# Three-stage kernel (attention, routed experts, gated convolution): one weight decoding, two decodings' last operations, one scaling and the routing's rest change place

## The chip, the cores and the metric

One core of a Trainium2 chip. The time is that of one execution on the device, in microseconds (us); the kernel before was run three times. The engines are TensorE (PE; PEld is its weight load), VectorE (DVE), ScalarE (ACT), GpSimd (POOL) and SyncE (SP, which only issues DMAs here). Each engine takes its instructions in the order of the program; engines wait for one another by semaphores.

## The reference

Three stages over 2 sequences of 768 tokens, 512 wide:

```python
state = gamma * state + outer(k[t], v[t]);  y[t] = scale * q[t] @ state      # 8 heads of 64
logits = x @ w_gate; local = sigmoid(x @ w_local)                             # 8 experts
e = argmax(logits[s]) if s == 0 or local[s] < 0.5 else prev_e                 # one expert per token
out[s] = softmax(logits[s])[e] * (relu(x[s] @ w1[e]) @ w2[e])                 # 512 -> 1024 -> 512
h = relu(x @ w_in); c = conv3(h, conv_w); y = (h * sigmoid(c)) @ w_out        # 512 -> 1024 -> 512
```

`w_in` and `w_out` arrive as 64-bit floats and have to be turned into 32-bit ones on the chip: the decoding. Matmuls are done as three products of split operands (a high and a low part of each; high x high, high x low, low x high).

## The kernel before, in words

The first stage goes over 12 tiles of 128 tokens and writes the tokens' rows to a scratch `scr` in DRAM; beside it the routing is worked out. In the second stage expert e gets 256 slots. Experts 1 to 6 run whole (`L1`, line 695, then `L2`, line 725); the first and the last run as two passes of 128 slots each (`alone`, line 629, a generator: each `yield` is a place at which the caller can put other work; n counts them). The third stage starts as soon as the rows of the first six tiles can be gathered.

Weights are loaded in units of 512 KB (`load_unit`, 4 buffers), split by a cast on ScalarE (line 172, `whi`) and a subtraction on VectorE (line 181, `wlo`), some 8 units ahead of their use. The subtraction's end lets SyncE issue the load that takes the buffer.

One decoding (`decode`, line 197; 16 in all) is: two reads on ScalarE (215, 216), five operations on VectorE (218 to 224), two on GpSimd (226 a product, 227 a sum). `dec_first` issues the two reads, `dec_second` the rest and then the next load of 64-bit data. The buffers `dmag`, `df` and `ds` exist once; decodings called with `mo` take others (`dmf`). 

The routing's rest (`route_rest`, line 549) is a generator of five pieces of 3 to 4 small VectorE operations, one piece with an exponential on ScalarE; it gives `posi`, the rows that the third stage gathers, and `G_all`, the factors by which it scales them (`c_scale`, on ScalarE for tile 4, on VectorE for tiles 0 to 3 and 5).

The order is written out by hand, instruction by instruction. Around the change it is: in the first expert's first pass the overflow's branch (line 836, not taken here), the gathers of expert 1, and the transposes T of the first expert's second half (lines 579 to 585: transposes on TensorE, cast `xsh` on ScalarE, subtraction `xsl` on VectorE). In the last expert's second pass the third stage's gathered tiles are scaled (`c_scale`), transposed and split (`c_T`, line 946) between the matmuls.

Of the kernel before, what the change touches and what calls it, by code (L numbers as in the profile page):

```python
# [8 lines left out]
F32 = mybir.dt.float32  # L9
# [5 lines left out]
ALU = mybir.AluOpType  # L15
# [5 lines left out]
DM = 512  # L21
# [76 lines left out]
def tile_kernel(ctx: ExitStack, tc: tile.TileContext, consts, qk, kv, w1, w2, w_in, conv_w, w_out, out):  # L98
    nc = tc.nc
# [94 lines left out]
    n_dec = KD + KF // 2  # L194
    wdec = [(dp if j < n_dec - KEPT else cst).tile([P, 1024], F32, name=f"wdec{j}") for j in range(n_dec)]

    def decode(raw64, out, pool=None, s=None):

        n, m = out.shape
        r3 = raw64.rearrange("p (c two) -> p c two", two=2)  # L200
        lo, hi = r3[:, :, 0], r3[:, :, 1]

        def tmp(name, dt):
            return dp.tile([P, DM], dt, name=name, tag=name)[0:n, 0:m]

        if pool is None:
            mag, f = tmp("dmag", F32), tmp("df", F32)
        else:
            both = pool.tile([P, 2, DM], F32, name="dmf", tag="ow", bufs=2)
            mag, f = both[0:n, 0, 0:m], both[0:n, 1, 0:m]  # L210
        s = (tmp("ds", F32) if s is None else s[0:n, 0:m]).bitcast(I32)
        a = mag.bitcast(I32)
        ve = nc.vector

        nc.scalar.activation(out=mag, in_=hi.bitcast(F32), func=AF.Abs)
        nc.scalar.activation(out=f, in_=lo.bitcast(U32), func=AF.Copy, scale=2.0 ** -52)
        yield
        ve.tensor_scalar(mag, mag, F64_LOW, F64_HIGH, op0=ALU.max, op1=ALU.min)
        ve.tensor_scalar(a, a, 4, -2 ** 31, op0=ALU.logical_shift_left, op1=ALU.bitwise_xor)
        yield  # L220
        ve.tensor_scalar(s, hi, -2 ** 31, None, op0=ALU.bitwise_and)
        ve.scalar_tensor_tensor(out=a, in0=a, scalar=1, in1=s, op0=ALU.logical_shift_right, op1=ALU.bitwise_or)

        ve.tensor_scalar(s, a, -2 ** 23, None, op0=ALU.bitwise_and)  # L224
        yield
        nc.gpsimd.tensor_tensor(out=f, in0=f, in1=s.bitcast(F32), op=ALU.mult)  # L226
        nc.gpsimd.tensor_tensor(out=out, in0=f, in1=a.bitcast(F32), op=ALU.add)  # L227

    dec_src = []
    for dt in range(KD):  # L230
# [4 lines left out]
    dec_raw = {}  # L235
# [8 lines left out]
        queue.dma_start(out=t, in_=dec_src[u].bitcast(I32))  # L244
        dec_raw[u] = t

    def dec_first(pool=None, s=None):
        dec_second()
        u = dnx["run"]
        if u >= len(dec_src):  # L250
            return
        dnx["run"] += 1
        dec_raw["g"] = decode(dec_raw.pop(u), wdec[u // 2][:, (u % 2) * DM:(u % 2 + 1) * DM], pool, s)
        next(dec_raw["g"])

    def dec_second(queue=nc.sync):
        if "g" in dec_raw:
            for _ in dec_raw.pop("g"):
                pass
            dec_load(queue)  # L260
# [17 lines left out]
    x0 = cst.tile([P, DM], F32, name="x0")  # L278
# [154 lines left out]
    last = {"cnt": base}  # L433
# [169 lines left out]
    def moe(mo):  # L603
# [11 lines left out]
        def T(e, halves=(0, 1)):  # L615
            if e not in xs_t:
                xs_t[e] = (mo.tile([P, KD, CAP], F32R, name="xsh", tag="xsh", bufs=1),
                           mo.tile([P, KD, CAP], F32R, name="xsl", tag="xsl", bufs=1))
            for half in halves:
                sl = slice(half * P, (half + 1) * P)  # L620
                transposed(xg_t[e].pop(half), *(x[:, :, sl] for x in xs_t[e]))
# [73 lines left out]
        def L1(e):  # L695
            xh, xl = xs_t.pop(e)
            hh, hl = h_tiles(e)
            pb = [bank("b") if j < 3 else std for j in range(KF // 2)]
            for dt in range(KD):
                wh, wl = split[e * 8 + dt]  # L700
                if dt == 0:
                    dec_second()
                elif dt == 1:
                    next(rest, None)
                elif dt == 2:
                    dec_first(mo)
                for ft in range(KF):
                    o = pb[ft // 2][:, (ft % 2) * CAP + OFF:(ft % 2 + 1) * CAP]
                    fs = slice(ft * P, (ft + 1) * P)

                    for n, (a, b_) in enumerate(((wh, xh), (wl, xh), (wh, xl))):
                        nc.tensor.matmul(o, lhsT=a[:, fs], rhs=b_[:, dt, OFF:], start=(dt == 0 and n == 0 and ft % 2 == 0),  # L712
                                         stop=(dt == KD - 1 and n == 2), skip_group_check=True)
                    if dt == KD - 1 and ft % 2:
                        fp = ft // 2
                        dst = hh[:, 2 * fp:2 * fp + 2, OFF:]
                        pair = pb[fp].rearrange("p (a t) -> p a t", a=2)[:, :, OFF:]
                        nc.scalar.activation(out=dst, in_=pair, func=AF.Relu)  # L718
                        nc.vector.scalar_tensor_tensor(out=hl[:, 2 * fp:2 * fp + 2, OFF:], in0=pair, scalar=0.0,  # L719
                                                       in1=dst.bitcast(F32), op0=ALU.max, op1=ALU.subtract)  # L720
                split.pop(e * 8 + dt)
                if dt < KD - 1:
                    split_unit(nc.vector)
# [53 lines left out]
            pass  # L777
        rest = route_rest()
        for n, _ in enumerate(first):
            if n in (0, 1, 2, 5):  # L780
                split_unit(nc.vector)
            if n == 5:
                T(0, (1,))
            if n == 3:
                overflow(mo)
                gather(1)
            if n == 5:
                dec_first()
            elif n == 7:
                dec_second()  # L790
        for n, _ in enumerate(alone(0, 1, True)):
            if n == 0:
                dec_first()
            elif n == 1:
                dec_second()
            if n == 9:
                T(1, (0,))
            elif n == 11:
                T(1, (1,))
                gather(2)  # L800
# [10 lines left out]
        for n, _ in enumerate(alone(e, 0, False)):  # L811
            if n in (0, 8, 13):
                dec_second()
            elif n == 5:
                dec_first()
            elif n == 9:
                dec_first(mo, x0)
        raw0 = [dp.tile([P, 2, DM], F32, name="yg0", tag="draw", bufs=2) for _ in range(2)]
        ygs = [raw0[c // 2][:, c % 2, :] for c in range(4)] + [x_last.rearrange("p a t -> p (a t)"), x0]
        for c in range(NC):  # L820
# [2 lines left out]
        for n, _ in enumerate(alone(e, 1, True)):  # L823
            if 8 <= n < 12:
                c_scale(n - 8)
            if n == 7:
                window(1, [wp.tile([P, 1024], F32R, name="x2", tag=tag) for tag in ("whi", "whi", "wlo", "wlo")])
            if 10 <= n < 14:
                c_T(0, n - 10, "ab"[n % 2])
            if n == 12:  # L830
                c_scale(4)
            if n == 13:
                c_scale(5)

    def overflow(mo):
# [413 lines left out]
```

## Time and profile before

| | |
|---|---|
| median of 3 runs | 410.25 us (409.18 to 411.04) |
| the profiled execution's own time | 409.37 us |
| its span, first to last instruction | 407.6 us |
| mean granted TensorE clock | 0.996 |
| TensorE busy | 391.4 us (96%) |
| VectorE busy | 286.8 us (70%) |
| ScalarE busy | 246.6 us (60%) |
| GpSimd busy | 117.8 us (29%) |

TensorE is busy nearly all of the span, the others are not; so the table says little of which of them matters where. For that one looks at the few stretches in which TensorE stands still, and at the granted clock in them. Times in the rows below are us from the span's start.

### The profile page before, as it was taken

To read this page: it belongs to the slowest core of one execution; us is meant where nothing else is said; L and a number is where in the kernel's file an instruction comes from. 1 tells how busy PE (TensorE), PEld (TensorE's weight loads), DVE (VectorE), ACT (ScalarE), POOL (GpSimd) and SP (SyncE) were. 2 spreads that over 40 slices of the span, in tenths; PEclk is the share of its full clock that TensorE was granted. 3 is DMA by queue.
4 is the path that set the end of the run, shared out by engine and by line. 5 is a ranking of instruction groups with operands and counts; after the bars stand their busy time and mean duration, and the time that the engine had idled before them with its cause. 6 is when DMAs were issued, how large, how long until landed. Compare 5 with 4: busy or idle time off the path is not lost.

```text
span 407.6 us, 7354 instructions
## 1 busy us (share of the span) xinstructions
PE 391.4 (96%) x2772; PEld 339.0 (83%) x2772; DVE 286.8 (70%) x544; ACT 246.6 (60%) x483; POOL 117.8 (29%) x110
## 2 busy tenths in 40 slices
PE   7999998979999999999999999799999999999996
PEld 4888876658989797998989777599979889998986
DVE  3368867957797999987877857659963736991350
ACT  4887752646855766576757563478864537981431
POOL 3455510264035153564744246532000000000000
PEclk9999999989999999999999999999999999999999
DMA  8999992868878797988979130533010010001002
GB/s 289 396 351 407 325 347 92 239 232 284 308 244 277 270 318 255 290 298 277 304 246 304 53 101 26 156 90 92 0 51 27 0 54 27 2 0 51 27 0 77
DMA packets 28087, 73.24 MB, mean 180 GB/s; under 512 B 3009, under 2 KB 3649, under 8 KB 28050
## 3 DMA queue, kind: packets, MB, share of 16 engines
q1 hardware_dynamic: 19506, 54.67, 39.1%
q10 hardware_dynamic: 6240, 10.55, 7.2%
q0 software_dynamic: 2304, 7.54, 6.0%
q8 instruction: 22, 0.36, 0.4%
q14 instruction: 15, 0.12, 0.1%
HBM read 62.26 MB, written 10.49 MB: 178 GB/s over the span
## 4 chain that ended last, share of the span: by engine, by line
PE 66%; DVE 17%; ACT 6%; DMA 5%; issue 4%; POOL 1%; ACTq 0%; DVEq 0%; POOLq 0%
PE c L1045 15%; PE b L993 11%; PE c L744 11%; DVE wlo L181 6%; PE rt L993 5%; PE b L712 4%; PE c L406 2%; PE b L652 2%; PE state L712 2%; PE rt L712 2%; PE b L346 2%; ACT whi L172 2%; DMA raw<-in_moe_w_dram 2%; PE a L374 2%; DMA C<-in_consts_dram 1%
## 5 line engine op out<-in xcount | busy, mean ns | idle before, releaser
L181 DVE TENSOR_TENSOR wlo<-raw,whi 128x1024 fp32r<-128x1024 f32 x64 | 82.1, 1295 | 18.4 <-ACT whi L172 17.6
L172 ACT CAST whi<-raw 128x1024 fp32r<-128x1024 f32 x64 | 66.7, 1055 | 40.6 <-PE c L744 21.9
L1012 DVE SCALAR_TENSOR_TENSOR cs<-hs,cw,cs 128x384 f32<-128x384 f32 x64 | 39.6, 619 | 30.6 <-ACT cs L1010 29.0
L226 POOL TENSOR_TENSOR dmf<-dmf,ds 128x512 f32<-128x512 f32 x12 | 24.9, 2076 | 83.5 <-DVE ds L224 50.1
L744 PE MATMUL c<-whi,hh 128*112 128x512 f32 x96 | 38.0, 395 | 0.3 <-ACT hh L718 0.3
L993 PE MATMUL b<-x,whi 128*128 128x386 f32 x176 | 37.1, 340 | 0.8 <-ACT x L960 0.8
L744 PE MATMUL c<-wlo,hh 128*112 128x512 f32 x96 | 37.5, 390 | 0.0
L1045 PE MATMUL c<-whi,gh 128*128 128x512 f32 x88 | 35.1, 399 | 0.0
L1045 PE MATMUL c<-whi,gl 128*128 128x512 f32 x88 | 34.9, 396 | 0.0
L1045 PE MATMUL c<-wlo,gh 128*128 128x512 f32 x88 | 34.7, 395 | 0.0
L993 PEld LDWEIGHTS b<-x,whi 128*128 128x128 f32 x176 | 31.2, 189 | 1.4 <-ACT x L960 1.2
L744 PE MATMUL c<-whi,hl 128*112 128x512 f32 x96 | 29.8, 392 | 0.6 <-DVE hl L719 0.6
L611 POOL DMA_INDIRECT xg<-scr,permi x15 | 20.3, 1353 | 26.5 <-DVE nbi L541 19.6
L712 PE MATMUL b<-xsl,whi 128*128 128x240 f32 x96 | 26.6, 277 | 0.4 <-DVE xsl L585 0.4
L712 PE MATMUL b<-xsh,whi 128*128 128x240 f32 x96 | 26.5, 276 | 0.0
L712 PE MATMUL b<-xsh,wlo 128*128 128x240 f32 x96 | 26.4, 275 | 0.0
L352 DVE TENSOR_TENSOR A<-b,mask 128x512 f32<-128x512 f32 x24 | 15.4, 685 | 11.1 <-PE b L346 11.1
L227 POOL TENSOR_TENSOR wdec<-dmf 128x512 f32<-128x512 f32 x13 | 22.8, 1757 | 1.0
L1016 ACT ACTIVATE sg<-cs 128x384 f32<-128x384 f32 x32 | 16.6, 519 | 9.1 <-DVE gl L1022 8.5
L744 PEld LDWEIGHTS c<-whi,hl 128*112 128x112 f32 x96 | 17.2, 181 | 5.8 <-DVE hl L719 1.5
L744 PEld LDWEIGHTS c<-whi,hh 128*112 128x112 f32 x96 | 17.4, 181 | 4.9 <-ACT hh L718 0.6
L744 PEld LDWEIGHTS c<-wlo,hh 128*112 128x112 f32 x96 | 17.4, 181 | 4.2
(251 smaller groups left out, 1015.9 us busy)
## 6 DMA issues: line engine op xcount, KB each, us to landing
raw<-in_moe_w_dram SPq DMA_DIRECT2D x64, 512.0 KB, 4.8
qk<-in_qk_dram SPq DMA_DIRECT2D x11, 512.0 KB, 6.6
kv<-in_kv_dram SPq DMA_DIRECT2D x11, 512.0 KB, 6.6
draw<-in_moe_w_in_dram SPq DMA_DIRECT2D x8, 512.0 KB, 3.6
draw<-in_moe_w_out_dram SPq DMA_DIRECT2D x8, 512.0 KB, 3.3
scr<-xo ACTq DMA_DIRECT2D x11, 256.0 KB, 8.1
out_dram<-os ACTq DMA_DIRECT2D x11, 256.0 KB, 2.0
scr<-ys ACTq DMA_DIRECT2D x10, 256.0 KB, 4.2
```

What stands on the lines that cost most here:

```text
L172: nc.scalar.copy(hi, raw[u])
L181: engine.tensor_tensor(out=lo, in0=t, in1=hi.bitcast(F32), op=ALU.subtract)
L226: nc.gpsimd.tensor_tensor(out=f, in0=f, in1=s.bitcast(F32), op=ALU.mult)
L227: nc.gpsimd.tensor_tensor(out=out, in0=f, in1=a.bitcast(F32), op=ALU.add)
L352: nc.vector.tensor_tensor(out=A_t[i][j], in0=sc2[j].rearrange("p (a t) -> p a t", a=NP), in1=mask.unsqueeze(1).to_broadcast([P, NP, P]), o ...
L611: nc.gpsimd.indirect_dma_start(out=t, out_offset=None, in_=xrow, in_offset=bass.IndirectOffsetOnAxis(ap=permi[:, col:col + 1], axis=0))
L712: nc.tensor.matmul(o, lhsT=a[:, fs], rhs=b_[:, dt, OFF:], start=(dt == 0 and n == 0 and ft % 2 == 0), stop=(dt == KD - 1 and n == 2), skip ...
L744: nc.tensor.matmul(yp[t][0:P - o], lhsT=a[:, ft, t * P + o:(t + 1) * P], rhs=b_[:, ws], start=(ft == 0 and a is hh and b_ is wh), stop=(ft ...
L993: nc.tensor.matmul(pb[:, 0:WN], lhsT=split[u_in + dt][wi][:, fs], rhs=x_[dt // 2][:, dt % 2, :], start=(n == 0), stop=(n == 3 * KD - 1))
L1012: nc.vector.scalar_tensor_tensor(out=cs, in0=tap[j], scalar=cw[:, j, ft:ft + 1], in1=cs, op0=ALU.mult, op1=ALU.add)
L1016: nc.scalar.activation(out=sg, in_=cs, func=AF.Sigmoid)
L1045: nc.tensor.matmul(ops[t][:, 0:n_], lhsT=a[:, ts_], rhs=b_[:, ws], start=(ft == 0 and n == 0), stop=(ft == KF - 1 and n == 2))
```

## The change

`decode` gets an argument `last`, the engine of its two last operations (226 and 227): GpSimd unless said otherwise, VectorE for the two decodings of the last expert's first pass. In the first expert's first pass the first decoding's reads are issued at n = 3 behind the gathers instead of at n = 5 behind T, its other operations at n = 4 instead of n = 7, and the split that stood at n = 5 now stands at n = 7; T stays at n = 5. `L1` no longer runs a piece of the routing's rest; `L2` does as before. In the last expert's second pass the scaling of tile 4 moves from n = 12 to n = 13, behind the transposes and casts of that step; the scaling of tile 5 stays at n = 13.

```diff
-    def decode(raw64, out, pool=None, s=None):
+    def decode(raw64, out, pool=None, s=None, last=nc.gpsimd):
...
-        nc.gpsimd.tensor_tensor(out=f, in0=f, in1=s.bitcast(F32), op=ALU.mult)
-        nc.gpsimd.tensor_tensor(out=out, in0=f, in1=a.bitcast(F32), op=ALU.add)
+        last.tensor_tensor(out=f, in0=f, in1=s.bitcast(F32), op=ALU.mult)
+        last.tensor_tensor(out=out, in0=f, in1=a.bitcast(F32), op=ALU.add)
...
@@ L1
                 if dt == 0:
                     dec_second()
-                elif dt == 1:
-                    next(rest, None)
                 elif dt == 2:
                     dec_first(mo)
...
@@ first expert, first pass
         for n, _ in enumerate(first):
-            if n in (0, 1, 2, 5):
+            if n in (0, 1, 2, 7):
                 split_unit(nc.vector)
-            if n == 5:
-                T(0, (1,))
             if n == 3:
                 overflow(mo)
                 gather(1)
-            if n == 5:
                 dec_first()
-            elif n == 7:
+            elif n == 4:
                 dec_second()
+            elif n == 5:
+                T(0, (1,))
...
@@ last expert, first pass
             elif n == 5:
-                dec_first()
+                dec_first(last=nc.vector)
             elif n == 9:
-                dec_first(mo, x0)
+                dec_first(mo, x0, nc.vector)
...
@@ last expert, second pass
-            if n == 12:
+            if n == 13:
                 c_scale(4)
-            if n == 13:
                 c_scale(5)
```

## Rows read from the trace of the kernel before

**Rows 1.** TensorE's waits, whole span: who waited for whom, us, times, longest.
```profile
PE a L640 <- ACT hr L663: 3.2, 2, 3.0
PE a L950 <- DVE yg L942: 2.5, 1, 2.5
...
PE c L744 <- DVE hl L719: 0.6, 2, 0.5
```

**Rows 2.** Timeline, TensorE, first expert: start, duration, operation, [idle before, releaser].
```profile
79.40 0.50 PE L652 MATMUL b<-whi,xsl 128*128 128x512 f32 x1
79.74 0.39 PE L652 MATMUL b<-whi,xsh 128*128 128x512 f32 x1
...
86.38 0.66 PE L640 MATMUL a<-ident,hr 128*128 128x128 f32 x4 [2.99 <-ACT hr L663]
...
90.42 0.72 PE L640 MATMUL a<-ident,hr 128*128 128x128 f32 x4
```

**Rows 3.** Two stretches: busy PE, PEld, DVE, ACT, POOL; clock; DMA share; GB/s.
```profile
88.00:90.00 2.00, 2.00 (x7) 1.51 (x5) 1.75 (x2) 1.20 (x2) 1.92 (x2) 0.50 0.71 242
256.00:260.00 4.00, 1.54 (x9) 0.88 (x7) 2.04 (x4) 1.02 (x3) 3.13 (x3) 1.00 0.70 197
```

**Rows 4.** Timeline, the other engines, first expert.
```profile
78.60 0.96 POOL L611 DMA_INDIRECT xg<-scr,permi  x1 [0.30 <-issue]
78.66 0.68 DVE L585 TENSOR_TENSOR xsl<-a,xsh 128x512 fp32r<-128x512 f32 x1
79.26 0.55 DVE L218 TENSOR_SCALAR dmag<-dmag 128x512 f32<-128x512 f32 x1
...
81.97 1.29 POOL L226 TENSOR_TENSOR df<-df,ds 128x512 f32<-128x512 f32 x1 [2.40 <-DVE ds L224]
...
84.62 0.66 ACT L215 ACTIVATE dmag<-draw 128x512 f32<-128x512 f32 x1 [5.98 <-POOL wdec L227]
...
89.25 2.14 POOL L227 TENSOR_TENSOR wdec<-df,dmag 128x512 f32<-128x512 f32 x1
```

**Rows 5.** Timeline, TensorE: transposes T behind L1 of experts 1 to 4.
```profile
108.19 1.04 PE L582 MATMUL a<-ident,xg 128*128 128x128 f32 x8
...
130.82 1.03 PE L582 MATMUL a<-ident,xg 128*128 128x128 f32 x8
...
154.47 1.03 PE L582 MATMUL a<-ident,xg 128*128 128x128 f32 x8
...
177.82 1.04 PE L582 MATMUL a<-ident,xg 128*128 128x128 f32 x8
```

**Rows 6.** Timeline, VectorE and ScalarE: third piece of the rest, expert 2.
```profile
126.98 1.35 DVE L565 TENSOR_TENSOR ex<-LG,MX 128x96 f32<-128x96 f32 x1
...
128.37 0.28 ACT L566 ACTIVATE ex<-ex 128x96 f32<-128x96 f32 x1 [4.74 <-DVE ex L565]
```

**Rows 7.** DMA busy tenths, 40 equal slices of 248.1:253.7.
```profile
DMA  0000003999940000000000000000000000000000
```

**Rows 8.** Timeline, all engines, around the start of the third stage; last row: first stage.
```profile
252.28 1.30 POOL L227 TENSOR_TENSOR wdec<-dmf 128x512 f32<-128x512 f32 x1
253.73 0.98 POOL L968 DMA_INDIRECT yg<-scr,posi  x1
...
255.60 0.69 DVE L644 TENSOR_TENSOR hl<-a,hh 128x512 fp32r<-128x512 f32 x1 [0.61 <-ACT hh L643]
258.25 0.49 DVE L942 TENSOR_SCALAR yg<-yg,G_all 128x512 f32<-128x512 f32 x1 [1.96 <-DMA yg<-scr,posi]
...
264.92 0.73 ACT L944 ACTIVATE x_last<-x_last,G_all 128x512 f32<-128x512 f32 x1
...
265.76 0.44 PE L993 MATMUL b<-x,whi 128*128 128x386 f32 x1 [0.81 <-ACT x L960]
...
9.17 0.69 DVE L325 TENSOR_TENSOR qk<-qk,wdec 128x512 f32<-128x512 f32 x1 [1.06 <-ACT wdec L316]
```

**Rows 9.** The chain that ended last: start, us, what.
```profile
96.86 6.79 DMA raw<-in_moe_w_dram
```

More of the change, by code (lines that the diff above doesn't have):

```diff
@@ L245, in dec_load, with dec_first @@
         dec_raw[u] = t
-    def dec_first(pool=None, s=None):
+    def dec_first(pool=None, s=None, last=nc.gpsimd):
         dec_second()
@@ L252, in dec_first @@
         dnx["run"] += 1
-        dec_raw["g"] = decode(dec_raw.pop(u), wdec[u // 2][:, (u % 2) * DM:(u % 2 + 1) * DM], pool, s)
+        dec_raw["g"] = decode(dec_raw.pop(u), wdec[u // 2][:, (u % 2) * DM:(u % 2 + 1) * DM], pool, s, last)
         next(dec_raw["g"])
```

## The prediction

> **What bounds the kernel now.** I read first who TensorE waits for over the whole span, then its timeline around each long wait, then the timelines of the engines that it waited for. [rows 1] shows two waits that stand out, 3.0 us for a ReLU result `hr` at line 640 and 2.5 us for a scaled gather at line 950, and two short ones for `hl` at line 744. TensorE is otherwise fed, so a saving counts only where it shortens one of these waits, and from the last stage's first matmul (265.8) on the list has no wait of TensorE at all, so what is gained before it stays gained.
>
> The first wait is in the second half of the first expert. [rows 2] has the end of it at 86.38, 2.99 us after TensorE ran dry. The cause is three engines away [rows 4]: ScalarE's queue held the reading part of the second decoding (line 215) in front of that `hr`, and this one stood 5.98 us because the first decoding's sum (line 227 on GpSimd, which reads the same single buffer `dmag`) ended only at 84.6; hr came 1.76 us behind that (84.62 to 86.38). The idle stretch also cost clock: [rows 3] has the granted clock at 0.50 in 88 to 90 (1.2 of 2.4 GHz), against 1.00 after the 2.5 us wait at 256 to 260. In [rows 2] nine matmuls stand between the transposes of 86.38 and those of 90.42. The transposes issue for 0.41 us, so the nine took 3.63; at the 0.233 us each at which matmuls follow one another from 79.74 on they would take 2.10. So 1.5 us more.
>
> **Part 1, the first decoding moved up.** It goes from behind the second-half transposes T to ahead of them; one weight split (cast on ScalarE, subtraction on VectorE) goes from ahead of T to near the end of that pass. Instructions and bytes stay the same: 2 ScalarE, 5 VectorE and 2 GpSimd operations, and one DMA load on SyncE, which is now issued ahead of one weight load instead of behind it (that weight's cast comes over 10 us later, so I price this at nothing).
> VectorE: the five operations took from 79.26 to about 81.9, when GpSimd took over [rows 4], so 2.6 us. In the new order they start when VectorE is through the branch of the overflow, at 77.5 (before, the split began about there and `xsl` followed at 78.66). In just that stretch two gathers run on GpSimd, the second from 78.60 to 79.56, the first, as long, 1.24 ahead of it. The row of line 218 shows what this does: it began at 79.26 inside the second gather, took 0.55 us where nothing else held it, and ended 0.25 after the gather. I read it as waiting for the gather's end. The Trainium skill says the same of the port pair that both engines share (SBUF — State Buffer, "Who interferes with whom": the one that starts second is blocked for the whole instruction, not slowed); four of the five are of the kind that it names, so it speaks against putting them there. By the rule alone both gathers would block, and the last of the three cases below would hold.
> Unhindered the five would end at 80.0, with one wait at 80.7, with both at 81.6. I take 80.9, between the last two. `xsl` (0.68) is now behind them: 81.6 instead of 79.34. TensorE's third matmul of the second half (79.40 in [rows 2]) needs it and stalls 2.2 us, a wait that is new. Sixteen matmuls later, 3.8 us, it is at 85.4.
> GpSimd: the pair of 226 and 227 took 81.97 to 84.6 alone; the moved split's subtraction now runs beside it, and [rows 4] shows what that costs at 89.25: 2.14 instead of 1.29. From 80.9 the pair ends at 83.7 to 84.6; I take the late end, as the row with that company does. Then `hr` comes at 86.4 as before: that wait shrinks from 3.0 to about 1.0 us, but its end does not move. What is gained is the clock: two idle stretches of 2.2 and 1.0, each shorter than the 2.46 us after which the clock stayed at 1.00. Of the 1.5 us I leave 0.3 to the next wait, since at full clock TensorE comes sooner to the second ReLU, and ScalarE has a cast ahead of that. **1.2 us**; from below, -1.3 (rival 4), from above 2.9 (rival 1).
>
> **Part 2, the routing's rest leaves L1.** Its five pieces ran at L1 and L2 of experts 1 to 3; they now run at L2 of experts 1 to 5. [rows 5] gives the period of an expert from T to T: 22.63 us for the first, then 23.65 and 23.35. The excess is 1.0 and 0.7 us, and in both a wait of line 744 for `hl` is in it (two in [rows 1]): VectorE, in order, came late to `hl`, since in these two L1 stages it also ran a piece of the rest. One operation of it took 1.35 us for 96 elements per lane, beside GpSimd's product of a decoding, and ScalarE stood 4.74 us for it before its exponential [rows 6], with the next cast behind that. Without the pieces `hl` is ready at least 1.3 us sooner, more than each excess. The pieces at L2 cost VectorE the same, where only splits used many microseconds later are behind them; at expert 3 the exponential holds ScalarE's casts about 2.6 us, which the later experts' slack covers (period of 22.6). **1.7 us**, between 0 (the weights' chain stays the bound) and 1.7, as there is no more waiting to remove; if the cover fails, -0.7 for pieces that now wait on GpSimd and did not before.
>
> **Part 3, the last two decodings on VectorE.** Removed: four GpSimd operations, the last ending at 253.58 [rows 8]; the first gather of the next stage started right behind, at 253.73. Added: four VectorE operations of 0.69 each [rows 8], the 512-element product on VectorE at 9.17: 2.8 us. VectorE was done with its five where GpSimd's last pair began, 1.4 ahead of 252.28; with all 2.8 on top it ends at 253.7, ahead of the `hl` of 255.60 that the first scaling follows. What holds the gather next: the store of the first half's rows. Its DMA row [rows 7] covers 248.1 to 253.7 in 40 slices of 0.14 us; its traffic ends in the twelfth, 249.8, so the rows have landed by about 250.3. The gather starts 3.4 us sooner and lands, 4.5 later as before (253.73 to 258.25), near 254.8. But the scaling at 258.25 cannot follow that far: the `hl` ends at 256.29, and TensorE, which waited 2.5 us for the end of that scaling [rows 1], comes there only at 256.2. So 1.95 at most; gathers and scalings meet again on the shared port, up to one gather (0.95) per scaling. I take **1.5**; bounds 0 (the gather waits for something not in these rows) and 1.95.
>
> **Part 4, the scaling of the fifth tile.** Only one of the two moves: it goes behind the cast of the two columns for which the window's first matmul waits. ScalarE spent 0.73 there (264.92) directly ahead of that cast, and TensorE waited 0.81 [rows 8]. VectorE's subtraction of the previous tile, through 264.8, is next, so **0.5**, between 0 and 0.73. Its tile is transposed only behind the window's first dozen matmuls, so the new place is early enough.
>
> **Sum.** 1.2 + 1.7 + 1.5 + 0.5 = 4.9. The profiled execution took 409.37 (span 407.6, 1.8 around it), so about 404.5 for it; it lies 0.9 under the median of 410.25, from which I count: 405.4.
>
> **Rivals.**
> 1. The gathers don't hinder VectorE. Its five operations end at 80.0, GpSimd's pair at 82.9, `hr` at 84.7: 1.7 more in part 1, and part 3 at its full 1.95: 403.2. For it: one gather may be blocked by VectorE rather than the reverse. Against: the row at 79.26.
> 2. The weights take over. The chain that ended last runs through a 6.79 us load there [rows 9] and on through casts and subtractions, not through TensorE. If that chain keeps its hour, expert 1 starts earlier and waits there; parts 1 and 2 are lost, 3 and 4 stay: 408.2. Against: the load's trigger is a subtraction that itself hangs on the first expert, so it moves too.
> 3. Part 3 does not do what it says: the gather waits for the store, or `x0`, as long as before. 406.9.
> 4. Slower. GpSimd's gathers and VectorE's decoding block each other in turn, each gather stretched to 2 us, so that `xsl` ends at 83.6. The point from which it decides is an idle stretch of 3.0 us, `xsl` after 82.3: then the clock falls at once. TensorE idles 4.3, loses 1.5 to the clock, and is at the transposes at 88.9 instead of 86.4, without the slow stretch after it: 1.3 lost. The same blocking takes parts 2 (-0.7) and 3 (0, the gathers now run against VectorE's new operations, and `hl` waits for these): 412.2, part 4 being hidden behind it.
>
> **Chances.** The sum 0.56, its own range 403.4 to 407.4; rival 1 0.12, rival 2 0.15, rival 3 0.07, rival 4 0.10. A measurement of this kernel tells 0.5% (2 us) from no change. Faster: the sum, rivals 1 and 3, and half of rival 2, less a little for what I don't see, 0.76. Same: the other half, and part of rival 4, 0.15. Slower 0.09. The range leaves out rival 4 and the outer edges of 1 and 2: 402.8 to 409.2.
>
> **What would show it.** Part 1: a wait of TensorE at the third matmul of the second half of about 2 us, line 640's wait about 1, granted clock 1.00 from 84 to 92. Part 2: periods near 22.6 for experts 2 and 3. Part 3: the first gather at about 3 us after the store's issue, the wait at line 950 under 1 us. Part 4: under 0.4 us ahead of the window's first matmul. The prediction is wrong if the clock falls in the first expert all the same, or if line 712 or 744 wait for weights.

## The result, and the profile after

The changed kernel took 404.17 us (median of 4 runs, 403.58 to 404.91) against 409.72 for the kernel before on the same chip (4 runs, 409.07 to 411.04): ratio 0.9866, 95% interval 0.9847 to 0.9886. The forecast was 405.4, with a range of 402.8 to 409.2. The profiled execution of the changed kernel took 404.91, span 403.1, mean granted clock 1.000 (before 0.996). In it lines up to 702 keep their numbers; 712, 718, 719, 744, 942, 950, 960, 963, 968 and 993 of before are 710, 716, 717, 742, 938, 946, 956, 959, 964 and 989.

TensorE's waits over the whole span (who waited for whom: us, times, longest), to be held against [rows 1]:

```profile
PE a L640 <- ACT hr L663: 1.3, 2, 1.0
...
PE c L742 <- DVE hl L717: 0.5, 2, 0.4
...
PE rt L946 <- DVE yg L938: 0.5, 1, 0.5
```

Both long waits are gone: 3.0 for `hr` became 1.0 and a new 1.0 for `xsl`, 2.5 for the first scaled gather became 0.4, and 0.5 for the fourth is new. The wait for `hl`, of which part 2 was to be rid, is nearly as long as before in this execution; in a second one (a_again below) the list has none. The two stretches of [rows 3] (columns as there):

```profile
88.00:90.00 2.00, 1.96 (x13) 1.37 (x13) 1.81 (x2) 1.25 (x3) 1.92 (x2) 1.00 0.50 166
...
256.00:260.00 4.00, 3.54 (x21) 2.80 (x22) 3.34 (x7) 2.15 (x5) 1.31 (x2) 1.00 0.62 181
```

The clock is 1.00 (2.4 GHz) where it was 0.50: 13 matmuls in 88 to 90 instead of 7.

To see which part gave what, I cut each profiled execution at the same points of TensorE's timeline: the second-half transposes T of the first expert (T0), the start of L1 of expert 1, the transposes T behind L1 of experts 1 and 5 (T1, T5; [rows 5]), and from those of expert 6 (T6) the first transposes of gathered rows and the last stage's first matmul. Before T0 the executions differ by up to 1.0 us (76.03 to 77.08) for reasons that are not the edits', so the stretches are compared and not the points themselves. From the last stage's first matmul to the end of the span all but one take 141.7 to 142.0 us.

| stretch, us | before | after | after, run again | forecast |
|---|---|---|---|---|
| T0 to expert 1 (part 1) | 20.47 | 18.29 | 18.29 | -1.2 |
| T1 to T5 (part 2) | 92.28 | 92.01 | 91.12 | -1.7 |
| T6 to first gathered rows (part 3) | 35.67 | 33.61 | 33.60 | -1.5 |
| from there to the last stage's first matmul (part 4) | 6.97 | 6.72 | 6.63 | -0.5 |

The four gains are 2.18, 0.27, 2.06 and 0.25: 4.8, as 4.9 was forecast, but by other shares. In the second execution they are 2.18, 1.16, 2.07 and 0.34: 5.8. So one kernel differs by 0.9 us in the stretch of part 2 from one execution to the next, and a single profile does not tell what that part is worth.

**Part 1.** VectorE, ScalarE and TensorE of the changed kernel in the first expert (start, duration, operation, [idle before, releaser]), then GpSimd; before: [rows 2, 4].

```profile
77.58 0.43 DVE L218 TENSOR_SCALAR dmag<-dmag 128x512 f32<-128x512 f32 x1 [0.22 <-DVEq L833]
...
79.57 0.43 DVE L224 TENSOR_SCALAR ds<-dmag 128x512 int32<-128x512 int32 x1
79.92 0.68 DVE L585 TENSOR_TENSOR xsl<-a,xsh 128x512 fp32r<-128x512 f32 x1
80.52 2.25 DVE L181 TENSOR_TENSOR wlo<-raw,whi 128x1024 fp32r<-128x1024 f32 x1
...
83.40 0.34 ACTq L689 DMA_DIRECT2D scr<-ys  x1
83.95 0.66 ACT L215 ACTIVATE dmag<-draw 128x512 f32<-128x512 f32 x1 [5.31 <-POOL wdec L227]
...
80.65 0.50 PE L652 MATMUL b<-whi,xsl 128*128 128x512 f32 x1 [1.04 <-DVE xsl L585]
85.70 0.66 PE L640 MATMUL a<-ident,hr 128*128 128x128 f32 x4 [1.05 <-ACT hr L663]
```

```profile
77.54 1.04 POOL L611 DMA_INDIRECT xg<-scr,permi  x1 [3.81 <-DVEq L833]
78.89 1.47 POOL L611 DMA_INDIRECT xg<-scr,permi  x1 [0.30 <-issue]
80.38 1.29 POOL L226 TENSOR_TENSOR df<-df,ds 128x512 f32<-128x512 f32 x1
81.75 2.17 POOL L227 TENSOR_TENSOR wdec<-df,dmag 128x512 f32<-128x512 f32 x1
```

The gather had started 0.04 us ahead of line 218, and this one took 0.43, less than its 0.55 of [rows 4]. The five ended at 80.0, not 80.9; `xsl` was there at 80.6, not 81.6, and TensorE stood 1.04 instead of 2.2. It was the gathers that gave way (1.04 and 1.47 instead of 0.94 and 0.96). Behind them the moved split and GpSimd's pair took turns: the product had started 0.14 us ahead of the subtraction and took its 1.29; the subtraction ended 1.10 behind it (2.25 instead of 1.22), and the sum ended 1.15 behind the subtraction (2.17 instead of 1.27). So `hr` came only 0.7 sooner than before, 0.9 counted from T0. The rest of the 2.2 us is clock: in p3_vector below, which has no edit here and in which the clock happened to stay at 1.00 behind the same wait, T0 to expert 1 took 19.15. That makes 1.3 for the clock and 0.9 for `hr`.

A gather can hold VectorE too, but only at its end. In p13_pair, which has the same order here:

```profile
78.22 0.95 POOL L611 DMA_INDIRECT xg<-scr,permi  x1 [3.76 <-DVEq L836]
...
78.77 0.65 DVE L219 TENSOR_SCALAR dmag<-dmag 128x512 int32<-128x512 int32 x1
```

Line 219 began 0.40 us before the gather's end and ended 0.25 behind it. Ten of the runs have such a row of lines 218 or 219: begun 0.23 to 0.40 us before the end of a gather, it took 0.47 to 0.65 and ended 0.24 to 0.26 behind it, as the 0.55 of [rows 4] did. Lines 218, 219, 221 and 224 begun earlier in a gather (0.5 us or more before its end) took 0.41 to 0.47.

**Part 2.** The transposes of [rows 5] in the changed kernel; their distances were 22.63, 23.65, 23.35 and are 22.76, 23.05, 23.28 (22.63, 22.66, 22.87 in the second execution):

```profile
106.19 1.04 PE L582 MATMUL a<-ident,xg 128*128 128x128 f32 x8
...
128.95 0.49 PE L582 MATMUL a<-ident,xg 128*128 128x128 f32 x3
...
152.00 0.38 PE L582 MATMUL a<-ident,xg 128*128 128x128 f32 x2
...
175.28 0.49 PE L582 MATMUL a<-ident,xg 128*128 128x128 f32 x3
```

VectorE and GpSimd ahead of the second of them (T2), then VectorE in the second execution:

```profile
124.77 5.68 DVE L181 TENSOR_TENSOR wlo<-raw,whi 128x1024 fp32r<-128x1024 f32 x3
...
124.98 2.15 POOL L226 TENSOR_TENSOR dmf<-dmf,ds 128x512 f32<-128x512 f32 x1 [4.75 <-ACT dmf L216]
127.21 2.15 POOL L227 TENSOR_TENSOR wdec<-dmf 128x512 f32<-128x512 f32 x1
...
130.37 1.21 DVE L717 SCALAR_TENSOR_TENSOR hl<-b,hh 128x480 fp32r<-128x480 f32 x2
```

```profile
124.14 5.67 DVE L181 TENSOR_TENSOR wlo<-raw,whi 128x1024 fp32r<-128x1024 f32 x3
129.73 1.21 DVE L717 SCALAR_TENSOR_TENSOR hl<-b,hh 128x480 fp32r<-128x480 f32 x2
```

Where the rest's operations stood, three splits' subtractions now run into GpSimd's pair, by turns with it: 5.68 us for three, where the same three take 3.49 without GpSimd beside them (a_vec_L below). From the first of these subtractions to `hl` it is 5.6 us in both executions and in experts 2 and 3 alike; before, it was 7.0 in expert 2 and 6.0 in expert 3. So VectorE gained 1.4 us ahead of `hl` in the one and 0.4 in the other.

The two executions differ in how late VectorE gets there: `hl` begins 1.4 us behind T2 in one and 0.6 in the other. It is so from expert 1 on, where a cast on ScalarE stood longer for a load of weights in the first execution than in the second (L1 of expert 1 began at 94.69 and 94.99):

```profile
98.22 1.05 ACT L172 CAST whi<-raw 128x1024 fp32r<-128x1024 f32 x1 [3.36 <-DMA raw<-in_moe_w_dram]
```

```profile
97.12 1.05 ACT L172 CAST whi<-raw 128x1024 fp32r<-128x1024 f32 x1 [2.28 <-DMA raw<-in_moe_w_dram]
```

That this lateness is handed on from expert to expert is read from the order of the queues; no run tests it.

**Parts 3 and 4.** The changed kernel around the start of the third stage, against [rows 8]:

```profile
245.90 0.33 ACTq L689 DMA_DIRECT2D scr<-ys  x1
...
248.72 0.69 DVE L227 TENSOR_TENSOR wdec<-dmf 128x512 f32<-128x512 f32 x1
...
248.81 1.47 POOL L964 DMA_INDIRECT yg<-scr,posi  x1 [8.48 <-DVE dmf L226]
...
254.46 0.66 PE L946 MATMUL a<-ident,yg 128*128 128x128 f32 x4 [0.41 <-DVE yg L938]
...
261.18 0.97 PE L989 MATMUL b<-x,whi 128*128 128x386 f32 x4 [0.20 <-ACT x L956]
```

The first gather starts 2.9 us behind the issue of the store (line 689), before 5.6 (253.73 against an issue at 248.17). VectorE's last operation of the decoding (248.72 to 249.41) is well ahead of the `hl` that the scaling follows. Ahead of the last stage's first matmul 0.20 is left of 0.81.

### The profile page after: what moved, and what is told of

It is laid out like the page before. It is cut to its first block, busy times and chain, and to the rows that moved or that the text cites. A ratio compares the mean times of both kernels' runs of the same rounds, so it can differ in the third digit from the quotient of the medians.

```text
span 403.1 us, 7359 instructions
## 1 busy us (share of the span) xinstructions
PE 390.5 (97%) x2772; PEld 337.5 (84%) x2772; DVE 294.4 (73%) x548; ACT 246.7 (61%) x483; POOL 113.2 (28%) x106
## 4 chain that ended last, share of the span: by engine, by line
PE 55%; DVE 11%; issue 5%; DMA 5%; ACT 2%; POOL 2%; DVEq 0%; ACTq 0%; POOLq 0%
PE c L1041 15%; PE b L989 12%; PE c L742 11%; PE rt L989 5%; DVE wlo L181 5%; PE b L710 4%; DMA raw<-in_moe_w_dram 3%; PE state L710 2%; PE rt L710 2%; DVE hl L717 1%; DMA yg<-scr,posi 1%; ACT whi L172 1%; PE b L652 1%; PE a L946 1%; DVE xsl L585 1%
## 5 line engine op out<-in xcount | busy, mean ns | idle before, releaser
L181 DVE TENSOR_TENSOR wlo<-raw,whi 128x1024 fp32r<-128x1024 f32 x64 | 87.4, 1388 | 11.8 <-ACT whi L172 11.3
L227 POOL TENSOR_TENSOR wdec<-dmf 128x512 f32<-128x512 f32 x12 | 20.7, 1721 | 0.9
```

Source lines behind the costliest of these rows:

```text
L181: engine.tensor_tensor(out=lo, in0=t, in1=hi.bitcast(F32), op=ALU.subtract)
L227: last.tensor_tensor(out=out, in0=f, in1=a.bitcast(F32), op=ALU.add)
```

## The experiments

Medians stand beside those of the kernel before on the same chip; the ratio's 95% interval is in brackets.

**One part at a time.** Each is the kernel before with one part of the change.

```diff
# p1_order: the first expert's new order        # p2_rest: L1 without the rest's piece
-            if n in (0, 1, 2, 5):              -                elif dt == 1:
+            if n in (0, 1, 2, 7):              -                    next(rest, None)
...
# p3_vector: last two decodings                 # p4_scale: scaling of tile 4
+                dec_first(last=nc.vector)      -            if n == 12:
+                dec_first(mo, x0, nc.vector)   +            if n == 13:
```

> The kernel before with the first expert's new order alone. Theory A (the parts add up): the changed kernel reached the first matmul of line 712 of expert 1 2.0 us sooner than the kernel before (94.69 against 96.69), and nothing later gives it back, so about 2.0 us less, 407.7; granted clock 1.00 throughout 84 to 92, a wait of about 1.0 at the third matmul of the second half and one of about 1.0 at line 640. Theory B (the experts' chain keeps its hour): without the routing's rest moved out of L1, VectorE is as late to `hl` in experts 2 and 3 as before and the gain shrinks there; the transposes T of expert 5, at 200.5 before, come less than 1 us sooner, and the time is 409 or more.

> The kernel before without the routing's rest in L1, alone. Forecast on record: 1.7 us less (408.0), periods from T to T near 22.6 for experts 2 and 3. Theory L (the port that VectorE and GpSimd share): the piece of the rest only filled time in which VectorE was blocked by GpSimd's two operations of a decoding anyway; now the next weight subtractions are blocked there instead, some 2 us for three of them as in the changed kernel (5.68 us for three instead of 3.5), so periods of about 22.8, 23.1, 23.3, 22.9 and a gain of 0.5 us or less, 409.3.

> The kernel before with the last two decodings' last operations on VectorE, alone. Theory A: the first gather of the third stage starts about 3 us sooner relative to the store of the rows, the wait for the scaled gather shrinks from 2.5 to about 0.4, and 2.1 us go, 407.6. Rival: the later stage's subtractions and casts, which follow one another from tile to tile, are the bound there and take it back: the window's first matmul comes less than 1 us sooner, 409 or more.

> The kernel before with the scaling of tile 4 moved behind the casts of the next step, alone. Forecast on record: 0.5 us, the wait ahead of the window's first matmul from 0.81 to 0.3. Rival: VectorE's subtraction of the tile before lets the cast go no sooner than 0.25 us earlier; then 0.25 us, no difference in the times, and the cast of the two columns directly behind the other one.

| | median (before) | ratio | its own stretch, before 20.47 / 92.28 / 35.67 / 6.97 |
|---|---|---|---|
| p1_order | 408.42 (409.57) | 0.9975 [0.9961, 0.9990] | 18.29: -2.2 |
| p2_rest | 408.24 (409.57) | 0.9978 [0.9958, 0.9998] | 90.91: -1.4 |
| p3_vector | 408.33 (409.57) | 0.9972 [0.9956, 0.9989] | 33.61: -2.1 |
| p4_scale | 409.63 (409.57) | 1.0010 [0.9992, 1.0028] | 7.01: 0.0 |

In their stretches the first three parts do alone what they do in the whole, part 2 even more. In p2_rest the periods of experts 2 and 3 are both 22.66, although its three subtractions take 5.69 as well: the forecast 1.7 is there, and the theory that those subtractions would leave 0.5 or less is not borne out. The next period takes 0.3 of it back (22.94 instead of 22.65), as in every run with the pieces at L2 of expert 4 and the decodings' pair on GpSimd (22.92 to 22.97).

The medians give less, 1.2, 1.3, 1.2 and 0: 3.7 against the 5.5 of the whole. In each of the four at least one long wait stayed, and behind it the clock often fell: the mean granted clock of an execution was below 0.998 in 9, 9, 6 and 12 of their 12 (in the order of the table) and in 34 of the 35 of the kernel before beside them, but in none of the 8 of the changed kernel (4, and 4 of a_again). The length of the wait does not settle it. In p1_order TensorE and the clock (columns as in [rows 3]) behind the wait for the first scaled gather, shorter than the 2.46 of before behind which the clock had stayed:

```profile
256.65 0.97 PE L949 MATMUL a<-ident,yg 128*128 128x128 f32 x4 [2.10 <-DVE yg L941]
```

```profile
258.00:260.00 2.00, 2.00 (x9) 1.60 (x8) 1.86 (x5) 1.46 (x4) 1.50 (x2) 0.50 0.57 166
```

And the opposite, p3_vector behind the wait for `hr`, as long as the one of [rows 2] behind which it fell:

```profile
87.22 0.66 PE L640 MATMUL a<-ident,hr 128*128 128x128 f32 x4 [3.04 <-ACT hr L663]
```

```profile
88.00:90.00 2.00, 1.95 (x10) 1.27 (x8) 1.72 (x4) 1.94 (x3) 1.26 (x1) 1.00 0.66 199
```

Part 4 shows nothing alone because the clocks differ: in p4_scale the wait ahead of the window's first matmul is gone, but the clock was 0.53 in 260 to 262, behind a wait of 2.49 for the first scaled gather, where before it was 1.00. The fair comparison comes with the next run.

**Parts 1 and 3 together** (p13_pair), to see whether the missing 1.8 us were the clock behind the wait that each left.

> The kernel before with parts 1 and 3 together, without parts 2 and 4. Theory C (each part alone left one wait of 2 to 3 us in place, and in most executions the granted clock fell behind that wait, which the part's own gain does not show): with both long waits gone the clock stays at 1.00 and the parts give what their stretches showed in the traces, 2.2 and 2.1: the median 405.3, TensorE's clock 1.00 from 84 to 92 and from 256 to 262, the waits at lines 640 and 946/950 each under 1.3. Rival A (the parts only add up as they were timed one by one, -1.1 and -1.2): 407.2, and something other than the clock must be found for the rest of the change's 5.5.

406.66 against 409.81, ratio 0.9926 [0.9904, 0.9948]: 3.0 us (2.1 to 3.9), where the medians of the two alone gave 2.4 and the theory asked for 4.3. The clock was 1.00 throughout, and the two stretches show 18.29 and 33.60, the forecast 2.2 and 2.1. But T1 to T5 took 92.80, 0.5 more than before (92.34 in p1_order, 93.12 in p3_vector): with the pieces of the rest in L1 this stretch swings by nearly 1 us, and here against the gain. The swing is one wait in expert 2, and it is not for `hl`: TensorE stands for ScalarE's `hh`, which comes behind the exponential and the casts of [rows 6]. Before and in p3_vector:

```profile
132.20 0.48 PE L744 MATMUL c<-whi,hh 128*112 128x512 f32 x1 [0.34 <-ACT hh L718]
```

```profile
132.55 0.49 PE L744 MATMUL c<-whi,hh 128*112 128x512 f32 x1 [1.19 <-ACT hh L718]
```

The wait is 0.34, 0.37, 1.19, 0.56 and 0.86 in before, p1_order, p3_vector, p4_scale and p13_pair, and the period of expert 2 less this wait is 23.31 to 23.34 in all five. In none of the runs without the piece in L1 is it on the list. So part 2 also takes away this wait, whose length depends on the execution.

So the theory holds for the clock and falls for the sum, and the rival's 407.2 lies within the interval. Seen from here part 2 is worth 0.8 to 1.7 (92.80 to 92.01 and 91.12), and the medians leave 2.4 for parts 2 and 4 together. This run also gives part 4 its measure. It has no part 4, and the clock is 1.00 as in the changed kernel:

```profile
263.16 0.97 PE L992 MATMUL b<-x,whi 128*128 128x386 f32 x4 [0.81 <-ACT x L959]
```

The stretch of part 4 takes 7.24 here and 6.72 in the changed kernel, the wait 0.81 and 0.20: 0.5 us.

Some of the 1.8 us stays unexplained: in p1_order's profiled execution the last stage alone took 143.3 us, 1.5 more than elsewhere, and no edit is there.

**The changed kernel again, and with the decodings of experts 1 to 6 ended on VectorE** (a_again, a_vec_L).

```diff
-                    dec_first(mo)                       # L1 and L2
+                    dec_first(mo, last=nc.vector)
```

> The changed kernel once more, beside the others. If the parts only add up (1.0, 0.9, 1.2 and 0 us by their times alone), 3.1 us less than the kernel before, 406.5. If the parts help one another (each of the two long waits lets the clock fall in most executions, and the second part gives VectorE the room that the first needs), 5 us or more less, 404.2 as measured, and granted clock 1.00 in all stretches.

> The changed kernel with the last two operations of the decodings in L1 and L2 on VectorE too. Theory L (blocking on the shared port costs VectorE about 2 us per decoding): VectorE pays 1.4 us per decoding and is no longer blocked, the subtractions take 1.2 us each again, the waits for `hl` go, periods of 22.65 for experts 2 to 5, T of expert 5 some 1.3 us sooner, 402.9. Rival: VectorE is full in experts 1 to 3, so 1.4 us more per decoding make `hl` later; longer periods, 405 or more.

a_again 404.31, 0.9870 [0.9848, 0.9892] of 409.67: the change's gain again, more than the parts' single times add up to. a_vec_L 403.62, 0.9856 [0.9836, 0.9876]. In a_vec_L VectorE does 1.4 us more per decoding, and yet the three subtractions that took 5.68 take

```profile
125.00 3.49 DVE L181 TENSOR_TENSOR wlo<-raw,whi 128x1024 fp32r<-128x1024 f32 x3
```

and each of the four periods from T1 to T5 is 22.65 or 22.66 (90.61 in all, against 92.01). So without GpSimd's pair nothing is left of the waits in part 2's stretch, and that is shown. That the pair alone makes them is not: a_again and p2_rest have it too, with the same 5.67 and 5.69, and are only 0.5 and 0.3 us behind (91.12 and 90.91). The time is at most a little better: the two intervals overlap.

The Trainium skill (SBUF — State Buffer, "Who interferes with whom") says that a VectorE instruction with two operands in SBUF contends with a GpSimd instruction that reads SBUF, and that the one that issues first keeps the shared ports to its end. The trace agrees for the moved split: 1.22 alone, 2.25 behind line 226 that had started 0.14 us ahead of it, and line 227 then stood until the subtraction had ended. For line 218, which I had counted among those that a gather blocks, the trace does not agree: 0.43, ended 0.57 us ahead of a gather that had started first.

**The stall that I had forecast** (a_pool2): two more GpSimd products ahead of the first decoding's pair, results unused.

```diff
+                for _ in range(2):             # first expert, n == 4, ahead of dec_second
+                    nc.gpsimd.tensor_tensor(out=x0, in0=x0, in1=x0, op=ALU.subtract)
```

> The changed kernel with two extra GpSimd products of 128x512 (a buffer free at that time, minus itself) ahead of the first decoding's GpSimd pair. The pair and `hr` come 2.6 us later, so TensorE idles about 3.6 us at line 640. Clock theory: the granted clock falls to 0.50 behind it and expert 1 starts 3.8 us later (2.6 and 1.2), 408. Rival: the clock depends on something else than this idle stretch; it stays at 1.00 and expert 1 starts 2.6 us later, 406.8.

405.86, 0.9920 [0.9895, 0.9945]. VectorE and TensorE in a_pool2, and the clock:

```profile
79.45 1.42 DVE L224 TENSOR_SCALAR ds<-dmag 128x512 int32<-128x512 int32 x1
...
81.52 0.79 PE L652 MATMUL b<-whi,xsl 128*128 128x512 f32 x1 [2.29 <-DVE xsl L585]
```

```profile
82.00:84.00 2.00, 2.00 (x6) 1.52 (x6) 1.45 (x2) 0.00 (x0) 1.99 (x1) 0.50 0.92 342
```

The first of the two products (79.53 to 80.58) holds line 224 to 0.29 us behind its end: 1.42 instead of 0.43. The kernel before has the same in its last expert, lines 219 and 221 beside the pair: 1.40 and 1.51. So the wait at line 640 for which the run was made did not come (0.2), both forecast times were missed, and the stall stood at the third matmul instead. It is the stall of 2.2 us that my step had at this place, and for which it had the clock stay; here it takes the clock to 0.50, and T0 to expert 1 is 20.10, hardly less than before.

**T ahead of the five** (a_T_ahead): T in front of the first decoding's VectorE operations, its pair on VectorE, so that `xsl` waits for nothing.

```diff
-                dec_first()                    # n == 3
-            elif n == 4:
-                dec_second()
+                dec_first(last=nc.vector)
...
+            elif n == 6:
+                dec_second()
```

> The changed kernel with the first decoding's VectorE operations behind the transposes T of the second half and its last two on VectorE. Theory A: no wait at the third matmul of the second half; the sum ends near 82.2, `hr` at 84.0 and its wait is 0.8; expert 1 starts 1.6 us sooner and the time is 402.6. Rival (the weights keep their hour): the casts of experts 1 and 2 wait that much longer for their loads, T of expert 5 comes less than 0.5 us sooner, 404.

406.03, 0.9909 [0.9892, 0.9926]: slower than the change, which neither theory had. The sum ended at 82.9, yet the read for which `hr` waits began at 85.03:

```profile
83.93 0.68 DVE L687 COPY ys<-c 128x512 f32<-128x512 f32 x1
...
84.65 0.33 ACTq L689 DMA_DIRECT2D scr<-ys  x1
85.03 0.66 ACT L215 ACTIVATE dmag<-draw 128x512 f32<-128x512 f32 x1 [5.70 <-DVE ys L687]
...
86.79 1.12 PE L640 MATMUL a<-ident,hr 128*128 128x128 f32 x4 [2.90 <-ACT hr L663]
```

Ahead of it in ScalarE's queue stands the store of `ys` (line 689), and that waits for VectorE's copy, which is behind everything put on VectorE here. One undivided idle stretch of 2.90 us was left, and the clock was at 0.50 from 86 to 92.

**The second decoding's reads behind the ReLU** (b_reads_late on the kernel before; c_hr_first on a_vec_L, with T ahead of the five too).

```diff
-            if n == 0:                         # first expert, second pass
+            if n == 3:
                 dec_first()
-            elif n == 1:
+            elif n == 7:
                 dec_second()
```

> The kernel before with one edit: in the first expert's second pass the second decoding's two reads on ScalarE are issued at n = 3, behind the first ReLU, instead of at n = 0, and its other operations at n = 7 instead of n = 1. Nothing of the first decoding is moved. Theory H (the 3.0 us wait at line 640 is ScalarE's queue order: the ReLU stands behind a read that waits for GpSimd's sum): the ReLU runs as soon as TensorE has its block, at about 83.5 instead of 85.7, the transposes of line 640 start at about 84.2 instead of 86.4, no clock fall there, expert 1 starts 3.3 to 3.8 sooner; 406.0. Rival V (the five VectorE operations, now at n = 7, stand ahead of the second subtraction hl and of the splits there, 2.6 us): the wait moves to the products of line 671, and 1 to 1.5 us stay of the gain: 408.2.

> The changed kernel with the decodings of experts 1 to 6 ended on VectorE as in a_vec_L, the first decoding's five VectorE operations behind T (its reads stay at n = 3 ahead of T), and the second decoding's reads at n = 3 of the second pass, behind the first ReLU, its other operations at n = 7. Theory H: neither xsl nor the ReLU stands behind a decoding, so both waits of a_vec_L in the first expert (1.3 at the third matmul, 0.8 at line 640) go, the clock stays at 1.00, and the rest is as in a_vec_L: 403.6 - 2.0 = 401.6, expert 1 starting about 92.7. Rival V (the five at n = 7 hold the second hl and the next splits): a wait of 1 to 2 us at line 671 or in expert 1 takes the place: 403.0 to 403.6.

b_reads_late 411.40 against 409.81, 1.0042 [1.0023, 1.0061]; c_hr_first 407.27, 0.9938 [0.9914, 0.9962]. Both are slower than what they started from, and the cause of the wait is confirmed all the same. b_reads_late:

```profile
83.12 0.34 ACTq L689 DMA_DIRECT2D scr<-ys  x1
83.66 0.60 ACT L663 ACTIVATE hr<-b 128x512 f32<-128x512 f32 x1 [4.33 <-DVE ys L687]
...
84.31 0.66 PE L640 MATMUL a<-ident,hr 128*128 128x128 f32 x4 [0.23 <-ACT hr L663]
...
92.07 4.25 DVE L181 TENSOR_TENSOR wlo<-raw,whi 128x1024 fp32r<-128x1024 f32 x2
...
98.71 0.38 PE L712 MATMUL b<-xsl,whi 128*128 128x240 f32 x1 [2.85 <-DVE xsl L585]
```

```profile
100.00:102.00 2.00, 2.00 (x11) 2.00 (x11) 1.66 (x2) 1.05 (x1) 1.56 (x2) 0.50 0.92 256
```

(The last fence is the window in which the clock fell; columns as in [rows 3].) The 3.0 us wait for `hr` is gone (0.23), T0 to expert 1 falls from 20.47 to 18.56. But the second decoding, put off, now has its five operations and its GpSimd pair among the splits and the `xsl` of expert 1: two subtractions take 4.25, `xsl` comes 2.85 us late, the clock falls to 0.50, and from L1's start to T1 it takes 15.55 us instead of 11.50: 4 us lost for 1.9 won. c_hr_first shows the same, 18.16 and 15.38. The rivals (a new wait behind the five) were right in kind; the place was expert 1, which only c_hr_first's had named beside line 671, and the price was more than either had said (411.40 and 407.27 against 408.2 and at most 403.6).

**Another buffer instead** (d_two_buf, on a_vec_L): the first decoding takes `dmf`, and T stands ahead of the five.

```diff
-                dec_first()                    # n == 3
-            elif n == 4:
-                dec_second()
+                dec_first(mo)
             elif n == 5:
                 T(0, (1,))
+                dec_second()
```

> As a_vec_L (403.6), with two edits in the first expert: the first decoding takes the other buffer (`dmf`, as the decodings called with `mo` do), and its five VectorE operations stand behind T's subtraction xsl instead of ahead of T. The second decoding stays at n = 0 and n = 1. Theory H (the ReLU is late only because the read ahead of it waits for the sum that reads the one dmag): the read at line 215 no longer waits for GpSimd, the ReLU runs at about 83.3, xsl ends at 78.5, both waits of a_vec_L in the first expert (1.3 and 0.8) go, and unlike in c_hr_first the second decoding's VectorE operations run in the gap ahead of hl and its GpSimd pair is over by 88.5, ahead of the two splits that it stretched to 4.25: expert 1 starts at about 92.7 without a new wait of 2.8 at line 710, 401.6. Rival W (the weights' loads and splits are the bound behind the first expert, as b_reads_late and c_hr_first lost 2.8 us there for an xsl behind splits): expert 1 starts earlier but waits for weights or xsl, and ends as in a_vec_L: 403.0 to 404.0.

404.23 against 409.82, 0.9868 [0.9840, 0.9896]: no better than a_vec_L, and expert 1 starts no sooner (18.37 behind T0), so neither theory came. `xsl` makes no wait any more, and the read no longer needs the sum, but it comes at the same time:

```profile
83.33 0.33 ACTq L689 DMA_DIRECT2D scr<-ys  x1
83.79 0.67 ACT L215 ACTIVATE dmag<-draw 128x512 f32<-128x512 f32 x1 [4.32 <-DMA raw<-in_moe_w_dram]
...
85.55 0.66 PE L640 MATMUL a<-ident,hr 128*128 128x128 f32 x4 [2.25 <-ACT hr L663]
```

The store of `ys` lets it go, 0.46 behind its issue, as in a_T_ahead (0.38). So at this point two releases stand almost together: GpSimd's sum (83.92 in the changed kernel) and the store (83.40 to 83.74). Taking one away leaves the other. That it is the store is read from the order of ScalarE's queue, in two runs; the profile names other releasers for the read (VectorE's copy, a load), and no run moves the store by itself.

## Why the prediction was right, and where it was not

The time came out 1.2 us under the forecast (404.17 against 405.4), inside the range, and the direction was right. Against the table's first execution the four terms are off by +1.0, -1.4, +0.6 and -0.25 and nearly cancel. That the sum fitted so well is luck: in the second execution, where part 2 gave 1.2, they add up to 5.8.

**Part 1, 1.2 forecast, 2.2 found.** The forecast was all clock, with `hr` no sooner than before. The clock gave 1.3 (20.47 against 19.15), so that was right; `hr` gave 0.9 more. The step that failed is "with one wait at 80.7, with both at 81.6. I take 80.9". "I read it as waiting for the gather's end" holds for the row from which it was read, and for nine rows like it; but from it I charged VectorE 0.7 to 0.9 us for a gather, where no such operation lost more than 0.22 (0.65 instead of 0.43) and in the changed kernel none lost anything. What does hold VectorE for its whole length is GpSimd's product (1.42 in a_pool2). So the five ended at 80.0, rival 1's leg, and with it the stall was 1.04. That the gather can be the one that is stretched, I had named and given 0.12. "I take the late end, as the row with that company does" was right: 2.17, which is why `hr` gained 0.9 and not the 1.7 of that rival.

That the stretches would be "each shorter than the 2.46 us after which the clock stayed at 1.00" came out right and was no reason. Behind idle stretches of 2.10 (p1_order), 2.29 (a_pool2) and 2.90 us (a_T_ahead) the clock fell, behind 2.25 (d_two_buf), 2.46 [rows 1, 3] and 3.04 (p3_vector) it did not. With the 2.2 us that I had forecast, the term might well have been lost; with two stretches of 1.3 or less it was not, in any of the five profiled executions that have such (the changed kernel twice, a_vec_L, p1_order, p13_pair). Nor is 3.0 us the point of decision that rival 4 took it for. What decides between 2 and 3 us, these runs do not show.

**Part 2, 1.7 forecast, 0.3 and 1.2 found in two executions, 1.4 alone.** Three steps failed. "in both a wait of line 744 for `hl` is in it" leaves out the larger wait of expert 2, 0.34 for `hh`, whose swing from 0.3 to 1.2 makes the term one of the execution. "Without the pieces `hl` is ready at least 1.3 us sooner" held in expert 2 (1.4 of VectorE's time) and not in expert 3 (0.4): VectorE's next work, the splits, now runs by turns with GpSimd's pair, 5.68 us instead of 3.49, a cost that the sum did not have. And "only splits used many microseconds later are behind them" put the pieces' new places at nothing, where the period of expert 4 grew by 0.3. Alone the two periods still came down to 22.66; in the whole, where expert 1 starts 2 us sooner, VectorE has less in hand, and how much depends on when the weights land (casts 3.36 and 2.28 late). A term worked out on the timeline of before is not the term behind another edit.

**Part 3, 1.5 forecast, 2.06 found in its stretch.** Gather 3 us behind the store's issue (2.9), wait under 1 us (0.41): right. Of the 2.06, 0.27 goes again in the next stretch: with part 3 and without part 4 it takes 7.24 (p13_pair) instead of 6.97, with a new wait of 0.38 for the fourth scaled tile. That leaves 1.8, inside the upper bound of 1.95. For collisions of gathers and scalings I had taken off 0.45: the gathers were stretched (1.47, 1.71 and 1.26 in the changed kernel), the scalings were not (0.48 or 0.49 each).

**Part 4, 0.5 forecast, 0.5 found** against p13_pair. The table's 0.25 holds the 0.27 that part 3 costs in this stretch, and p4_scale's 7.01 holds a fall of the clock. What is next is VectorE's subtraction, as the text said: in the changed kernel ScalarE's casts of the columns wait 0.82 for it (line 959).

**Rivals.** 1 was right about the five and wrong about the pair behind them. 2 (the weights keep their hour) did not come as a whole: counted from T0, expert 1 starts 2.2 us sooner and T5 comes 2.4 sooner; but the weights' lateness in expert 1 is where the two executions of the changed kernel part. In b_reads_late and c_hr_first expert 1 also started sooner and waited there, yet for `xsl` behind slow subtractions, and T1 came later than before, counted from T0 (34.1 and 33.5 us against 32.0), so it is not the chain's hour either. 3 is refuted by p3_vector's stretch. 4 had its mechanism (mutual blocking, then the clock) right for products, as a_pool2 shows, and its place wrong: the gathers were stretched to 1.04 and 1.47, not to 2.

## What to carry to other kernels

An operation moved in an in-order queue makes room for what is behind it; look at what that next operation will run beside, for it is there that a share of part 2's gain went. When a wait has one obvious releaser, look for the second one that comes just before it (here a store in the same queue), and price an edit to the second. Cut the traces at fixed points and compare stretches: that places edits of 1 us. But take more than one execution, for one stretch of one kernel differed by 0.9 us between two; and compare only stretches with the same clock, for a fall hid part 4.

## What the runs showed of the hardware

The granted clock after an idle stretch of 2.1 to 3.0 us was 0.50 or 1.00, in no order of length; so a saving in clock from removing such a wait is a mean over executions and cannot be read from one profile. In the first expert a fall cost 1.3 us (20.47 against 19.15).

A VectorE operation with a scalar (lines 218 and 219) ran at its 0.43 us beside a GpSimd gather, unless it began in the gather's last 0.23 to 0.40 us; then it ended 0.24 to 0.26 behind the gather (0.47 to 0.65). Of the gathers some grew, from 0.95 to between 1.04 and 1.47, beside VectorE's operations. Beside a GpSimd product the same kind of operation stood until 0.3 us behind the product's end (1.40 to 1.51), and VectorE subtractions of two operands and GpSimd's products went by turns (2.3 and 2.15 each instead of 1.2 and 1.3).
